# Moving two small TensorE groups in a recurrent attention step: the second selection of the new memory, and the masks of the second head half

## The chip, the core and the metric

The kernel runs on one NeuronCore of one Trainium2 chip. A core has a matrix engine (TensorE, "PE" in the profile, its weight loads "PEld"), three engines for elementwise work (VectorE "DVE", ScalarE "ACT", GpSimd "POOL"), a queue engine (SyncE "SP") that starts transfers, and two on-chip memories: SBUF, and PSUM, where matmuls put their sums. Each engine works through its own list of instructions in the order in which the program gives them; where one needs what another makes, it waits on a semaphore.

The metric is the time of one execution on the device, in microseconds. The trace is that of one further execution, taken with the hardware profiler.

## The reference

Two branches, mixed by a gate. Branch A is an attention layer over 2048 tokens with a recurrent memory: the tokens come in 64 segments of 32; each segment is preceded by 8 memory rows, and the layer's output for those 8 rows is the memory of the next segment. So the segments form a chain.

```python
for s in range(n_seg):                                   # 64
    xs = x[:, s * seg_len:(s + 1) * seg_len, :]          # 32 rows of 512
    h = jnp.concatenate([mem, xs], axis=1)               # 8 + 32 = 40 rows
    q = jnp.einsum('btd,dhe->bhte', h, Wq)               # 32 heads of 128
    k = jnp.einsum('btd,dhe->bhte', h, Wk)
    v = jnp.einsum('btd,dhe->bhte', h, Wv)
    scores = jnp.einsum('bhqe,bhke->bhqk', q, k) * scale
    scores = jnp.where(mask[None, None], scores, -1000000000.0)
    p = _softmax(scores, axis=-1)
    o = jnp.einsum('bhqk,bhke->bhqe', p, v)
    o = jnp.einsum('bhte,hed->btd', o, Wo)
    mem = o[:, :M, :]                                    # the next segment's memory
    outs.append(o[:, M:, :])
```

Branch B is a layer norm, a 512 x 1376 x 512 MLP with gelu, on the same tokens. The output is `g * a + (1 - g) * b` with `g = sigmoid(sum(x * gate_w))`. All tensors are bf16.

## The kernel before

**Two stages.** The first computes branch B for all tokens, block by block, and loads the attention's weights meanwhile; its result, already scaled by `1 - g`, goes to DRAM (`c_dr`). The second is a loop of 64 steps, one for a segment, written out in full. Four steps form a tile of 128 tokens: step `s` has tile `T = s // 4` and place `si = s % 4`. The order on every engine is that of the program text (`tc.manual_schedule()`); there is no planner. Some instructions are put off by hand: `act_q` holds casts for ScalarE and `dve_q` work for VectorE, and `flush` issues them at fixed places.

**What a step multiplies.** The activations are the stationary operand, 32 columns at a time, in one of four column tiles of the array; the weights stream past, 512 columns at a time. Four such matmuls, one for each column tile, are a **unit** (`qk_unit` L120, `v_unit` L139, `wo_group` L151). The stationary `hT` holds 24 of the segment's tokens and the 8 memory rows as `[128, KC, 32]`, with the 512 features in `KC = 4` blocks of 128. The other 8 tokens of each segment ("left") don't depend on the memory, so they are done for a whole tile ahead of time, as side work.

**A step in the order of TensorE:**

1. Projections: four groups (Q, K for the first half of the heads, then for the second) of four units each, one unit for each feature block `kc`, into PSUM banks `U[0]` to `U[3]` (L120). Unit `kc` needs block `kc` of `hT`. ScalarE casts each bank to `Tb` (L125), VectorE transposes it into `QT` or `KT` (L129).
2. `scores(s, 0)`: the scores of the first half of the heads, into `Sb[0]` in bank `SbF` (L257, L261), on top of masks that were put there earlier.
3. `mask_mm(1)`: four matmuls of 224 columns (L249) that put the masks of the second half into `Sb[1]` in bank `W`. The scores accumulate on them.
4. V's first half, four units into `X1` (L139), and the first unit of V's second half, into `X2`. ScalarE meanwhile takes the exponentials of the first scores (L693) and then copies `X1` out (L696).
5. `msum(0)`: sums over the leading columns of the exponentials (L268, L271); VectorE normalises them (L688, L689).
6. `scores(s, 1)`, onto the masks in `W`. ScalarE takes their exponentials in two parts (L681).
7. Two more units of V's second half, `msum(1)` (L268, L271), which needs the first of those two parts, the last unit of V, and ScalarE's copy of `X2` (L710).
8. `W1` side units, the column sums (`xsums`, L600), and `av` (L281, L286): exponentials times V. ScalarE copies the result out (`UT` L718, then `XR` L606).
9. `W2` side units, then `wo_pass`: eight units that multiply by Wo into bank `W` (L151). ScalarE copies the result to `w` in two halves of 256 columns (L633).
10. `mask_mm(0)`, `W3` side units, in some steps `out_sel`.
11. `new_mem`, twice. Each call is eight matmuls of 8 columns (L640) that pick the memory rows out of one half of `w` and turn them, and a VectorE copy of the result into two of the four blocks of the next `hT` (L642). The first call makes blocks 0 and 1 (bank `U[1]`), the second blocks 2 and 3 (bank `U[3]`).

The POOL engine multiplies the outputs of the tokens by their normalisation (L626) one step late; its factor comes back through DRAM. `wo_pass` of a step needs that product of the step before.

**Side work.** `side(T, si)` is a generator: `run(n)` issues `n` units of it, and a loop over `fill` issues the rest. At `si = 0` and `1` it is eight units of Q and K for the next tile's left tokens, at `si = 3` eight units of V for them, at `si = 2` the eight units of `wo_left` for the tile before. There is none at `si = 0, 1, 3` of the last tile and at `si = 2` of the first, so 60 steps have side work. `WS` gives `W1, W2, W3` as (3, 2, 0) for `si = 0` and (2, 2, 2) for the others; so three units, or two, are left when `new_mem` comes.

Of the kernel before, what the change touches and what calls it, by code (L numbers as in the profile page):

```python
# [27 lines left out]
def kernel(ctx, tc, A_x, A_mem0, A_Wq, A_Wk, A_Wv, A_Wo, A_seg_len, B_x, B_w1, B_b1, B_w2, B_b2, gate_w, out):  # L28
# [63 lines left out]
    def load_xT(T):  # L92
        xT = ew.tile([P, KC, P], BF16, tag="xT", bufs=3, name="xT")
        nc.sync.dma_start_transpose(out=xT[:], in_=x2[T * P:(T + 1) * P, :])
        xTs[T] = xT
# [7 lines left out]
    U = [lps.tile([P, 512], FP32, name=f"U{i}") for i in range(4)]  # L103
# [13 lines left out]
    def qk_unit(bk, G, t, hf, kc):  # L117
        h0, h1 = HF[hf]
        for j in range(4):
            nc.tensor.matmul(bk[32 * j:32 * j + 32, :], lhsT=G[:, kc, :], rhs=W5[t][:, kc, h0:h1, j, :],  # L120
                             start=(kc == 0), stop=(kc == KC - 1), tile_position=(0, 32 * j))

    def qk_cast(bk):
        Tb = ew.tile([P, 8, 32, 2], BF16, tag="Tb", bufs=3, name="Tb")
        nc.scalar.copy(out=Tb[:], in_=bk.rearrange("p (a b e) -> p a e b", a=8, b=2))  # L125
        return Tb

    def qk_tr(Tb, dst, hf, c0=0):
        nc.vector.transpose(out=dst[:, 8 * hf:8 * hf + 8, c0:c0 + 32, :].rearrange("p a r b -> p a (r b)").bitcast(FP32),  # L129
                            in_=Tb[:].rearrange("p a e b -> p (a e b)").bitcast(FP32))  # L130
# [6 lines left out]
    def v_unit(bk, G, vb, kc):  # L137
        for j in range(4):
            nc.tensor.matmul(bk[32 * j:32 * j + 32, :], lhsT=G[:, kc, :], rhs=Wv5[:, kc, 4 * vb:4 * vb + 4, j, :],  # L139
                             start=(kc == 0), stop=(kc == KC - 1), tile_position=(0, 32 * j))  # L140

    def v_out(V, vb):
        return V[:, 4 * vb:4 * vb + 4, :].rearrange("p i e -> p (i e)")
# [15 lines left out]
    def flush(q, n=1):  # L159
        for _ in range(min(n, len(q))):  # L160
            q.pop(0)()
# [17 lines left out]
    def vp_load(T, si):  # L179
        nc.sync.dma_start(VP[T % 2][:, si].rearrange("p v e -> p (v e)"), VLs[T][si:P:SPT].rearrange("p a v e -> p a (v e)"))  # L180
# [20 lines left out]
    def c_load(T):  # L201
        c = cw.tile([P, Dm], BF16, tag="c", name="c")
        nc.sync.dma_start(c[:], c_dr[T * P:(T + 1) * P, :])
        cs[T] = c
# [30 lines left out]
    def prep_h(s):  # L235
        T, si = divmod(s, SPT)
        nc.gpsimd.tensor_copy(out=hT[s % 3][:, :, 0:RIDE], in_=xTs[T][:, :, seg * si:seg * si + RIDE])
# [9 lines left out]
    def mask_mm(i2):  # L247
        for j in range(4):
            nc.tensor.matmul(Sb[i2][32 * j:32 * j + 32], lhsT=ident[:, 32 * j:32 * j + 32], rhs=Mk[:],  # L249
                             start=True, stop=True, skip_group_check=True, tile_position=(0, 32 * j))  # L250
# [315 lines left out]
    def run(n):  # L566
        for _ in range(n):
            next(fill, None)
# [5 lines left out]
    def side(T, si):  # L574
        gens = []
        if si == 2:
            if T >= 1:
                gens.append(wo_left(T - 1, X1))
        elif T + 1 < NT:
            gens = [[left_qk(T + 1, 0, 0, X1), left_qk(T + 1, 1, 0, X2)], [left_qk(T + 1, 0, 1, X1), left_qk(T + 1, 1, 1, X2)], [],  # L580
                    [left_v(T + 1, 0, X1), left_v(T + 1, 1, X2)]][si]
        return chain(*gens)
# [20 lines left out]
    def x_raw(s):  # L603
        XR = cw.tile([P, 4, NG, 32], BF16, tag="XR", name="XR")
        for j in range(4):
            nc.scalar.copy(out=XR[:, j], in_=U[j][:, 0:NG * 40].rearrange("p (i q) -> p i q", q=40)[:, :, 0:32])  # L606
        XRs[s] = XR
# [13 lines left out]
    def x_norm(s):  # L621
        T, si = divmod(s, SPT)
        XR, Rb = XRs.pop(s), Rbs.pop(s)[:].rearrange("p (c q) (h j) -> p h j c q", c=4, h=2)
        for out, o, a, b in ((UT[(s + 1) % 2], M, LEFT, 32), (UL[T % 2], LEFT * si, 0, LEFT)):
            for h in range(2):
                nc.gpsimd.tensor_tensor(out=out[:, :, 4 * h:4 * h + 4, o:o + b - a], in0=XR[:, :, 4 * h:4 * h + 4, a:b], in1=Rb[:, h, :, :, a:b], op=ALU.mult)  # L626
# [9 lines left out]
    def new_mem(w, hn, bk, k0):  # L636

        for k in (k0, k0 + 1):
            for c in range(4):
                nc.tensor.matmul(bk[32 * c:32 * c + 32, M * k:M * k + M], lhsT=w[:, k * P + 32 * c:k * P + 32 * c + 32], rhs=SelM[:],  # L640
                                 start=(k == k0), stop=True, skip_group_check=True, tile_position=(0, 32 * c))
        nc.vector.tensor_copy(out=hn[:, k0:k0 + 2, RIDE:32], in_=bk[:, M * k0:M * k0 + 2 * M].rearrange("p (k m) -> p k m", k=2))  # L642
# [3 lines left out]
    for s in range(nseg):  # L646
        T, si = divmod(s, SPT)
        last = s == nseg - 1
        hc, hn = hT[s % 3], hT[(s + 1) % 3]
        W1, W2, W3 = WS[si]  # L650
        fill = side(T, si)
        if s + 1 < nseg:
            prep_h(s + 1)
        if s >= 1:
            x_norm(s - 1)
        if si == 0 and T >= 2:
            c_load(T - 2)
        if si < 3:
            vp_load(T, si + 1)
        if last:  # L660
            c_load(T - 1)
            c_load(T)
        if si == 0 and T + 2 < NT:
            load_xT(T + 2)
        for n, (t, hf) in enumerate(((0, 0), (1, 0), (0, 1), (1, 1))):
            bk = U[n]
            for kc in range(KC):
                qk_unit(bk, hc, t, hf, kc)
            if n == 0:
                flush(act_q, 9)  # L670
                flush(dve_q, 9)
            qk_tr(qk_cast(bk[:]), (QT, KT)[t], hf, LEFT * (1 - t))
        V = cw.tile([P, NG, Dh], BF16, tag="V", name="V")
        E = cw.tile([P, NG, EW], BF16, tag="E", name="E")
        R = cw.tile([P, NG * 40], FP32, tag="R", name="R")
        Rs[s] = R
        xsum = SbF[:, 0:32 * NG].rearrange("p (i q) -> p i q", q=32)

        def exps(i2, x):
            c = slice(0, 40) if x else slice(40, EW)  # L680
            nc.scalar.activation(out=E[:, 4 * i2:4 * i2 + 4, c], in_=Sb[i2][:, :, c], func=ACTF.Exp, scale=scale)  # L681

        def msum(i2):
            sums(U[i2][:, 320:352].rearrange("p (i q) -> p i q", q=8), E[:, 4 * i2:4 * i2 + 4, :], 40, 48, 8, True)

        def mnorm(i2):
            r, e = RP[i2], E[:, 4 * i2:4 * i2 + 4, 40:56].rearrange("p i (a q) -> p i a q", q=8)
            nc.vector.reciprocal(out=r, in_=U[i2][:, 320:352])  # L688
            nc.vector.tensor_tensor(out=e, in0=e, in1=r.rearrange("p (i q) -> p i q", q=8).unsqueeze(2).to_broadcast([P, 4, 2, 8]), op=ALU.mult)  # L689

        scores(s, 0)
        mask_mm(1)
        nc.scalar.activation(out=E[:, 0:4, :], in_=Sb[0], func=ACTF.Exp, scale=scale)  # L693
        for kc in range(KC):
            v_unit(X1, hc, 0, kc)
        nc.scalar.copy(out=v_out(V, 0), in_=X1[:])  # L696
        v_unit(X2, hc, 1, 0)
        if not last:
            msum(0)
            mnorm(0)  # L700
        scores(s, 1)
        for i2 in range(2):
            exps(1, i2)
        for kc in range(1, 3):
            v_unit(X2, hc, 1, kc)
        if not last:
            msum(1)
            mnorm(1)
        v_unit(X2, hc, 1, 3)
        nc.scalar.copy(out=v_out(V, 1), in_=X2[:])  # L710
        if last:
            break
        run(W1)
        xsums(s, E)
        recip_x(s)
        av(s, V, E)
        for j in (0, 2, 1, 3):
            nc.scalar.copy(out=UT[s % 2][:, j, :, 0:M], in_=U[j][:, 0:NG * 40].rearrange("p (i q) -> p i q", q=40)[:, :, 32:40])  # L718
        x_raw(s)
        run(W2)  # L720
        prep_q(s + 1)
        w = wo_pass(UT[s % 2], 2)
        if s >= 1:
            ws[s - 1] = w
        mask_mm(0)
        run(W3)
        for _ in extra(T, si):
            pass
        new_mem(w, hn, U[1], 0)
        for _ in fill:  # L730
            pass
        new_mem(w, hn, U[3], 2)
        if si == 3 and T + 2 < NT:
            left_x(T + 2)
        flush(dve_q, 9)
        nc.vector.tensor_tensor(out=rmin[:, 0:RW], in0=rmin[:, 0:RW], in1=R[:, 0:RW], op=ALU.min)
        flush(act_q, 9)
# [163 lines left out]
```

## Time and profile before

| | us |
|---|---|
| median of 3 runs | 787.48 |
| lowest, highest | 785.29, 788.54 |
| profiled execution | 785.75 |
| its span | 784.0 |
| TensorE busy | 766.3 (98%) |
| ScalarE busy | 524.5 (67%) |
| VectorE busy | 341.2 (44%) |
| POOL busy | 278.8 (36%) |

The span goes from the first instruction of the profiled execution to its last; the execution's own time is 1.75 us longer. The loop of steps begins about 97 us into it. Busy times of TensorE are unions of matmuls whose ends are modelled: matmuls overlap, so a wait shorter than their tail does not show as idle time, and the starts of successive matmuls have to be read instead. A row of the timeline gives start, length (both in us), engine, line, operation, tiles, shape and the number of merged instructions; in brackets, where there is one, the idle time before it and what ended it.

### The profile page before, as it was taken

How to read it: one execution, taken by the hardware profiler on the slowest of the kernel's cores; microseconds unless marked ns; L12 is line 12 of the kernel's file. 1: busy time of each engine (PE TensorE's matmuls, PEld its weight loads, DVE VectorE, ACT ScalarE, POOL GpSimd, SP SyncE). 2: the span in 40 equal slices, each digit the busy share in tenths (PEclk: the TensorE clock that was granted, in tenths of full speed). 3: DMA queues.
4: the chain of work that ended last, by engine and by line, in shares of the span. 5: the costliest groups of instructions: out<-in, count | busy, mean ns of one | idle time of the engine just before them, and what ended most of it. 6: DMA issues, size and time to landing. Idle time of an engine off the chain costs nothing.

```text
span 784.0 us, 44302 instructions
## 1 busy us (share of the span) xinstructions
PE 766.3 (98%) x19673; PEld 416.6 (53%) x19687; DVE 341.2 (44%) x1235; ACT 524.5 (67%) x1439; POOL 278.8 (36%) x523
## 2 busy tenths in 40 slices
PE   7999999999999999999999999999999999999996
PEld 5666455555555555555555555555555555555553
DVE  5776244334334343434443433434343444434334
ACT  4666566667677676667667677766666767666663
POOL 4111034333344343344434424443334443342342
PEclk9999999999999999999999999999999999999999
DMA  6789311213121222212121212122221212221211
GB/s 199 271 256 387 119 57 61 74 61 88 61 61 62 78 71 77 72 58 74 49 88 61 88 62 74 60 67 70 78 72 57 80 43 88 62 80 62 67 63 44
DMA packets 53174, 70.61 MB, mean 90 GB/s; under 512 B 21289, under 2 KB 42898, under 8 KB 51442
## 3 DMA queue, kind: packets, MB, share of 16 engines
q1 hardware_dynamic: 51250, 64.84, 25.6%
q8 instruction: 156, 2.56, 1.3%
q0 software_dynamic: 784, 1.97, 0.7%
q10 hardware_dynamic: 944, 0.92, 0.4%
q14 instruction: 40, 0.33, 0.1%
HBM read 56.96 MB, written 4.45 MB: 78 GB/s over the span
## 4 chain that ended last, share of the span: by engine, by line
PE 87%; DVE 1%; issue 0%; ACT 0%; DVEq 0%
PE U L120 30%; PE X L139 18%; PE W L151 15%; PE X L120 7%; PE X L151 4%; PE U L281 3%; PE U L640 2%; PE U L268 1%; PE W L257 1%; PE SbF L257 1%; PE W L249 1%; PE SbF L600 1%; PE SbF L249 1%; PE U L286 1%; PE U L466 1%; PE U L221 0%
## 5 line engine op out<-in xcount | busy, mean ns | idle before, releaser
L626 POOL TENSOR_TENSOR UT<-XR,Rb 128x384 bf16<-128x384 bf16 x126 | 140.3, 1134 | 297.6 <-DMA Rb<-r_dr 237.6
L125 ACT CAST Tb<-U 128x512 bf16<-128x512 f32 x258 | 150.9, 585 | 86.6 <-PE U L120 85.6
L120 PEld LDWEIGHTS <-hT 128*32 128x32 bf16 x4096 | 98.3, 96 | 110.9 <-DVE hT L642 26.8
L139 PE MATMUL X<-Wv_sb,hT 128*32 128x512 bf16 x2048 | 145.7, 379 | 0.0
L120 PE MATMUL U<-Wq_sb,hT 128*32 128x512 bf16 x2048 | 139.9, 381 | 0.8 <-DVE hT L642 0.5
L120 PE MATMUL U<-Wk_sb,hT 128*32 128x512 bf16 x2048 | 132.7, 379 | 0.0
L151 PE MATMUL W<-Wo_sb,UT 128*32 128x512 bf16 x2080 | 124.8, 380 | 1.5 <-ACT UT L718 1.5
L642 DVE CAST hT<-U 128x16 bf16<-128x16 f32 x126 | 22.0, 175 | 222.7 <-PE U L640 222.4
L129 DVE STREAM_TRANSPOSE QT<-Tb 128x256 f32<-128x256 f32 x128 | 56.6, 443 | 78.4 <-ACT Tb L125 78.4
L151 PEld LDWEIGHTS <-UT 128*32 128x32 bf16 x2080 | 57.8, 96 | 57.7 <-issue 18.5
L606 ACT CAST XR<-U 128x256 bf16<-128x256 f32 x252 | 78.6, 438 | 0.0
L129 DVE STREAM_TRANSPOSE KT<-Tb 128x256 f32<-128x256 f32 x128 | 57.1, 446 | 44.5 <-ACT Tb L125 44.3
L633 ACT CAST w<-W 128x256 bf16<-128x256 f32 (+1 forms) x128 | 41.9, 378 | 46.5 <-PE W L151 46.5
L139 PEld LDWEIGHTS <-hT 128*32 128x32 bf16 x2048 | 53.1, 95 | 20.4
L618 POOL TENSOR_TENSOR racc<-racc,R 128x72 f32<-128x72 f32 x63 | 21.2, 336 | 111.7 <-PE U L286 79.3
L626 POOL TENSOR_TENSOR UL<-XR,Rb 128x128 bf16<-128x128 bf16 x126 | 60.3, 502 | 0.0
L718 ACT CAST UT<-U 128x64 bf16<-128x64 f32 x252 | 35.3, 227 | 28.3 <-PE U L286 28.3
L710 ACT CAST V<-X 128x512 bf16<-128x512 f32 x64 | 37.4, 585 | 22.3 <-PE X L139 22.1
L466 PE MATMUL U<-w_sb,hTm 128*128 128x512 bf16 (+1 forms) x163 | 49.2, 379 | 0.6
L696 ACT CAST V<-X 128x512 bf16<-128x512 f32 x64 | 37.4, 585 | 15.6 <-PE X L139 15.6
L460 PEld LDWEIGHTS <-w_sb 128*128 128x128 bf16 (+1 forms) x352 | 34.2, 101 | 20.3 <-issue 3.0
L640 PEld LDWEIGHTS <-w 128*32 128x32 bf16 x1008 | 20.7, 94 | 42.6 <-ACT w L633 29.3
(158 smaller groups left out, 1179.8 us busy)
## 6 DMA issues: line engine op xcount, KB each, us to landing
Rb<-r_dr SPq DMA_DIRECT2D x63, 512.0 KB, 3.8
Wv_sb<-in_A_Wv_dram SPq DMA_DIRECT2D x4, 1024.0 KB, 6.5
Wq_sb<-in_A_Wq_dram SPq DMA_DIRECT2D x4, 1024.0 KB, 7.0
Wk_sb<-in_A_Wk_dram SPq DMA_DIRECT2D x4, 1024.0 KB, 9.5
Wo_sb<-in_A_Wo_dram SPq DMA_DIRECT2D x4, 1024.0 KB, 15.0
VP<-VL SPq DMA_DIRECT2D x64, 64.0 KB, 3.2
c<-c_dr SPq DMA_DIRECT2D x16, 128.0 KB, 3.3
out_dram<-o SPq DMA_DIRECT2D x16, 128.0 KB, 2.1
```

Source lines behind the costliest of these rows:

```text
L120: nc.tensor.matmul(bk[32 * j:32 * j + 32, :], lhsT=G[:, kc, :], rhs=W5[t][:, kc, h0:h1, j, :], start=(kc == 0), stop=(kc == KC - 1), tile_ ...
L125: nc.scalar.copy(out=Tb[:], in_=bk.rearrange("p (a b e) -> p a e b", a=8, b=2))
L129: nc.vector.transpose(out=dst[:, 8 * hf:8 * hf + 8, c0:c0 + 32, :].rearrange("p a r b -> p a (r b)").bitcast(FP32), in_=Tb[:].rearrange("p ...
L139: nc.tensor.matmul(bk[32 * j:32 * j + 32, :], lhsT=G[:, kc, :], rhs=Wv5[:, kc, 4 * vb:4 * vb + 4, j, :], start=(kc == 0), stop=(kc == KC - ...
L151: nc.tensor.matmul(bk[32 * c:32 * c + 32, :], lhsT=U_[:, j, i, :], rhs=Wo_sb[:, 4 * i + j, :], start=(n == 0), stop=(n == NW - 1), tile_po ...
L466: nc.tensor.matmul(bp(blk, tt)[:], lhsT=hTm[blk % 2][:rows, fc, tt * P:(tt + 1) * P], rhs=w2_sb[:rows, fc, :], start=(fc == 0), stop=(fc = ...
L606: nc.scalar.copy(out=XR[:, j], in_=U[j][:, 0:NG * 40].rearrange("p (i q) -> p i q", q=40)[:, :, 0:32])
L626: nc.gpsimd.tensor_tensor(out=out[:, :, 4 * h:4 * h + 4, o:o + b - a], in0=XR[:, :, 4 * h:4 * h + 4, a:b], in1=Rb[:, h, :, :, a:b], op=ALU ...
L633: nc.scalar.copy(out=w[:, a:a + Dm // parts], in_=W[:, a:a + Dm // parts])
L640: nc.tensor.matmul(bk[32 * c:32 * c + 32, M * k:M * k + M], lhsT=w[:, k * P + 32 * c:k * P + 32 * c + 32], rhs=SelM[:], start=(k == k0), s ...
L696: nc.scalar.copy(out=v_out(V, 0), in_=X1[:])
L710: nc.scalar.copy(out=v_out(V, 1), in_=X2[:])
```

## The change

Two groups of TensorE instructions change their place in each step.

- The masks of the second half of the heads, `mask_mm(1)`, stood between the first scores and V's first half. They now stand behind V's first half, ahead of the first unit of V's second half.
- The second `new_mem` (blocks 2 and 3 of the next `hT`) stood behind all side units that were left. It now stands behind one of them; the rest follow it.

No instruction is added or taken away, and no operand changes. In steps without side work the second edit changes nothing.

```diff
         scores(s, 0)
-        mask_mm(1)
         nc.scalar.activation(out=E[:, 0:4, :], in_=Sb[0], func=ACTF.Exp, scale=scale)
         for kc in range(KC):
             v_unit(X1, hc, 0, kc)
+        mask_mm(1)
         nc.scalar.copy(out=v_out(V, 0), in_=X1[:])
         v_unit(X2, hc, 1, 0)
...
         new_mem(w, hn, U[1], 0)
+        run(1)
+        new_mem(w, hn, U[3], 2)
         for _ in fill:
             pass
-        new_mem(w, hn, U[3], 2)
         if si == 3 and T + 2 < NT:
             left_x(T + 2)
```

## The prediction, made before the changed kernel was run

> **What bounds the kernel now.** I read the page first, then the waits of the weight loads, then stretches of the timeline.
>
> ```profile
> span 784.0 us, 44302 instructions
> PE 766.3 (98%) x19673; PEld 416.6 (53%) x19687; DVE 341.2 (44%) x1235; ACT 524.5 (67%) x1439; POOL 278.8 (36%) x523
> ```
>
> TensorE carries the kernel: 98% busy, and no other engine is near. But busy PE is a modelled overlap, so small stalls between matmuls vanish in it. They show at the weight loads, which carry the semaphore waits:
>
> ```profile
> PEld L640 <- ACT w L633: 29.3, 66, 0.8
> PEld L120 <- DVE hT L642: 26.8, 66, 0.8
> ```
>
> Columns: total us, times, longest. Two waits come back in nearly each of the 64 steps: L640 (the selection of the new memory) waits for ScalarE's copy of w, and L120 (next step's projections) for VectorE's copy of the new memory into hT. Edit B touches just these; a third stall, at the place of edit A, shows further down. I looked at both places in time.
>
> **Edit B, the second selection earlier.** The end of step 28 and its neighbour, step 29, show both forms; first step 29 (tile 7, si = 1), where two side units stand between the two selections:
>
> ```profile
> 413.65 0.62 PE L120 MATMUL X<-Wk_sb,GL 128*32 128x512 bf16 x8
> 414.21 0.21 PE L640 MATMUL U<-SelM,w 128*32 128x8 bf16 x8
> 414.27 0.60 PE L120 MATMUL X<-Wk_sb,GL 128*32 128x512 bf16 x8
> 414.70 0.20 PE L640 MATMUL U<-SelM,w 128*32 128x8 bf16 x8
> 414.79 1.15 PE L120 MATMUL U<-Wq_sb,hT 128*32 128x512 bf16 x16
> 415.76 0.60 PE L120 MATMUL U<-Wk_sb,hT 128*32 128x512 bf16 x8
> ```
>
> Beside it, the weight loads of hT, VectorE's copies into hT and ScalarE's copies of w:
>
> ```profile
> 414.78 0.12 PEld L120 LDWEIGHTS <-hT 128*32 128x32 bf16 x8
> 415.32 0.12 PEld L120 LDWEIGHTS <-hT 128*32 128x32 bf16 x8 [0.41 <-DVE hT L642]
> ```
>
> ```profile
> 414.56 0.17 DVE L642 CAST hT<-U 128x16 bf16<-128x16 f32 x1 [3.10 <-PE U L640]
> 415.09 0.17 DVE L642 CAST hT<-U 128x16 bf16<-128x16 f32 x1 [0.36 <-PE U L640]
> ```
>
> ```profile
> 413.79 0.65 ACT L633 CAST w<-W 128x256 bf16<-128x256 f32 x2 [0.65 <-PE W L151]
> ```
>
> Read starts, not durations (the durations of matmuls overlap). The middle of the step gives the pace of an unhindered unit of four 512-wide matmuls:
>
> ```profile
> 408.03 0.27 PE L249 MATMUL W<-Mk,ident 128*32 128x224 bf16 x4
> 408.13 1.25 PE L139 MATMUL X<-Wv_sb,hT 128*32 128x512 bf16 x20
> 409.21 0.19 PE L268 MATMUL U<-E,BO 128*32 128x32 bf16 x4
> 409.24 0.19 PE L271 MATMUL U<-E,BO 128*32 128x32 bf16 x4
> 409.26 0.27 PE L257 MATMUL W<-QT,KT 128*32 128x40 bf16 x16
> 409.37 0.20 PE L261 MATMUL W<-QT,KL 128*32 128x64 bf16 x4
> 409.40 0.63 PE L139 MATMUL X<-Wv_sb,hT 128*32 128x512 bf16 x8
> 409.98 0.20 PE L268 MATMUL U<-E,BO 128*32 128x32 bf16 x4
> ```
>
> Five units from 408.13 to 409.21 make 0.216 us a unit. The 16 matmuls on the new hT should take 0.86; from 414.79 to 415.76 they take 0.97. The loss is the wait for hT's second half: the second selection starts at 414.70, its VectorE copy ends at 415.26, the load that needs it goes at 415.32, 0.06 later. After the edit one side unit stands between the selections: 414.27 + 0.216 = 414.49. Is the second half of w there? ScalarE's pair ends at 413.79 + 0.65 = 414.44, and with the same 0.06 for the signal 414.50: just in time. A step with no side units measures it directly:
>
> ```profile
> 128.67 0.12 PEld L640 LDWEIGHTS <-w 128*32 128x32 bf16 x8 [0.75 <-ACT w L633]
> 128.94 0.12 PEld L640 LDWEIGHTS <-w 128*32 128x32 bf16 x8 [0.15 <-ACT w L633]
> ```
>
> ```profile
> 129.25 1.05 PE L120 MATMUL U<-Wq_sb,hT 128*32 128x512 bf16 x16
> 130.12 0.39 PE L120 MATMUL U<-Wk_sb,hT 128*32 128x512 bf16 x4
> ```
>
> There the second selection follows 0.27 after the first, with nothing between; 414.21 + 0.27 = 414.48. So the new wait is zero, the margin about zero too. Then: selection 0.07 (414.21 to 414.27, rounded up, as its loads can't be fetched ahead), the last side unit 0.216, which ends at 414.78, exactly when hT's first half is ready (the load at 414.78 now), so the projections start at 414.79 as today. Their third unit comes at 415.22; hT's second half, by the first copy's lag (414.21 to 414.56, then 0.17, 0.06), at 414.49 + 0.58 = 415.07. No stall. The 16 matmuls take 0.87 instead of 0.97, as they do in the step without side units (129.25 to 130.12): **0.10 us** a step. Step 28 has si = 0: three units between the selections, after the edit one, and two behind:
>
> ```profile
> 403.61 0.82 PE L120 MATMUL X<-Wk_sb,GL 128*32 128x512 bf16 x12
> ...
> 405.31 0.60 PE L120 MATMUL U<-Wk_sb,hT 128*32 128x512 bf16 x8
> ```
>
> ```profile
> 405.59 0.58 ACT L125 CAST Tb<-U 128x512 bf16<-128x512 f32 x1 [0.47 <-PE U L120]
> ```
>
> Selection at 403.83, two units from 403.90 to 404.33, 16 matmuls to 405.19 instead of 405.31: **0.12 us**. Side units exist in 60 steps: si = 0, 1, 3 of the first 15 tiles, si = 2 of the last 15. 45 x 0.10 + 15 x 0.12 = **6.3 us**. Both ends: nothing if w's second half is 0.10 late; below nothing beyond that (the slower rival below); 7.9 at most if the projections also began without their 0.03 of delay (414.79 against 414.70 + 0.06; 60 x 0.13). I take 6.3: the step without side units shows both halves of it.
>
> What else moves: VectorE and ScalarE issue in the same order. The side tile's last cast starts some 0.06 later on ScalarE; what follows it there waits 0.47 for TensorE (the 405.59 row), so that's covered, and uncovered would cost those 0.06. No DMA, SP or POOL instruction is moved. The POOL product that wo_pass (L151) needs is early:
>
> ```profile
> 406.19 2.23 POOL L626 TENSOR_TENSOR UT<-XR,Rb 128x384 bf16<-128x384 bf16 x2 [4.27 <-ACT Tb L125]
> ```
>
> It ends at 408.42. wo_pass is eight units (1.73), and ScalarE copies its result from 413.79 on, so it starts before 412; about 3 us of cover, from which a step shorter by 0.2 takes little.
>
> **Edit A, the masks behind V's first half.** The same four matmuls take 0.10 (408.03 to 408.13), so on TensorE it is a swap: V's first half ends 0.10 earlier, L268 at 409.21 and the second scores at 409.26 stay. What it moves is ScalarE:
>
> ```profile
> 408.13 0.59 ACT L125 CAST Tb<-U 128x512 bf16<-128x512 f32 x1 [0.23 <-PE U L120]
> 408.61 0.36 ACT L693 ACTIVATE E<-SbF 128x224 bf16<-128x224 f32 x1
> 409.22 0.58 ACT L696 CAST V<-X 128x512 bf16<-128x512 f32 x1 [0.24 <-PE X L139]
> 409.70 0.43 ACT L681 ACTIVATE E<-W 128x64 bf16<-128x64 f32 x2
> 410.48 0.58 ACT L710 CAST V<-X 128x512 bf16<-128x512 f32 x1 [0.35 <-PE X L139]
> 411.47 0.56 ACT L718 CAST UT<-U 128x64 bf16<-128x64 f32 x4 [0.41 <-PE U L286]
> ```
>
> A 512-wide cast is followed 0.48 later by the next activation (408.13 to 408.61). V's copy at 409.22 is followed 0.48 later, with no idle time, by L681, the exps of the second half: ScalarE, not the scores, sets that start. And L681 is on the path: the two V units from 409.40 end at 409.83, but the sums L268 stand at 409.98, 0.15 late, waiting for E. With V's copy at 409.12, ScalarE is free at 409.60. When do the scores allow it? Their last matmuls (L261) start at 409.37 to 409.38. For the lag of such a 64-wide matmul to ScalarE I take av's last ones, to the copy L718 at 411.47 that waits for them:
>
> ```profile
> 411.12 0.27 PE L281 MATMUL U<-E,V 32*128 32x40 bf16 x16
> 411.23 0.20 PE L286 MATMUL U<-E,VP 32*128 32x64 bf16 x4
> ```
>
> From 411.23 to 411.47 is 0.24, so 409.62. L681 moves from 409.70 to 409.62: **0.08 us**. The sums move to 409.90 (0.07 of wait stays), V's last unit and its copy (410.48) with them. That copy ends at 411.06 and releases the second half of av at 411.12, so the gain isn't eaten there. It applies in the 63 steps before the last: **5.0 us**. Ends: zero, if something unseen sets L681; 0.095 a step or 6.0 if the cast alone does. A loss is excluded: nothing but the masks moves back, and they are done about 0.2 before the second scores.
>
> The Trainium skill (ScalarE: Activation LUTs, What ACT_TABLE_LOAD costs) has an activation with immediates at 186 + 0.833 N ns, back-to-back ones overlapping by 93: an estimate of 0.52 us for this cast where the rows have 0.48. By it L681 would come at 409.64 and edit A be worth 3.8 us; the rows decide.
>
> **The sum.** 6.3 + 5.0 = 11.3 us. The profiled execution took 785.75, so 774.4. It lies under the median of the other three, 787.48; from the mean of the four, 786.8, I get **775.5 us**.
>
> **Rivals.**
> Only B pays (L681 is held by something other than the cast): 786.8 - 6.3 = 780.5. Against: 0.48 twice and no idle time before L681.
> Only A pays (B's 0.10 is given back at the first scores, L257, by casts and transposes): 781.8. Against: the casts and transposes ahead of those scores wait for these projections (the 405.59 row: idle until TensorE), so they move along.
> Slower: the second selection waits for w. TensorE takes matmuls in order, so a late w holds the last side unit and all behind it. Each 0.01 us later than 414.49 costs 0.6 us in all; at 0.10 B is gone, and from 0.19 (11.3 / 60) on the kernel is slower; a copy behind one more 0.48 cast on ScalarE would give 0.48 - 0.19, times 60, 804 us. For it: the margin is nil. Against: the 0.27 of the bare step. The Trainium skill (TensorE: Matmul & The Clock Gate, Part 3: Packing small matmuls) says that matmuls start and end in strict program order; the rows agree, as the side unit behind L640 starts only at 414.27.
> No change: both edits lie beside the path. Against: the 0.97 and the 0.15 are stalls of TensorE itself.
>
> **How the numbers follow.** Both pay 0.75; only B 0.09; only A 0.07; no change 0.04; slower 0.05. A measurement can tell about 0.5%, 3.9 us; the first three are faster by more: 0.91, 0.04, 0.05. The low end takes the upper terms (6.0 + 7.9 from 786.8 is 772.9); the high end takes in both single cases: 772.5 to 781.9.
>
> **What would show it.** The 16 matmuls on hT at 0.87; the second L640 some 0.28 behind the first; the wait of L120 for hT falling from 26.8 to a few us; L681 0.08 closer to the scores; L268 0.08 earlier; the selections of two neighbouring steps 0.18 to 0.20 closer together. The prediction is wrong if L640's wait for w grows by several us, or if new waits appear at L257 or L281.

## The result, and the profile after

The changed kernel takes **779.97 us** (median of 6 runs, 779.49 to 782.41); the kernel before, run beside it, 786.99 (6 runs). The ratio is 0.9915, interval 0.9904 to 0.9926: 7.0 us less, where 11.3 were forecast. The time lies in the range given, but only because the range takes in the rivals' times: it stands at "only B pays" (780.5), not at the forecast of 775.5.

The profile's first lines, of the kernel after:

```profile
span 777.7 us, 44316 instructions
PE 761.1 (98%) x19687; PEld 420.3 (54%) x19687; DVE 345.1 (44%) x1235; ACT 529.5 (68%) x1439; POOL 278.7 (36%) x523
```

The profiled execution took 779.49, against 785.75 before. TensorE is still the bound, and again the starts have to be read.

**Edit B came out as worked out.** The timeline of TensorE at the end of step 29, and the loads and copies beside it:

```profile
411.31 0.62 PE L120 MATMUL X<-Wk_sb,GL 128*32 128x512 bf16 x8
411.88 0.22 PE L640 MATMUL U<-SelM,w 128*32 128x8 bf16 x8
411.94 0.39 PE L120 MATMUL X<-Wk_sb,GL 128*32 128x512 bf16 x4
412.15 0.21 PE L640 MATMUL U<-SelM,w 128*32 128x8 bf16 x8
412.21 0.39 PE L120 MATMUL X<-Wk_sb,GL 128*32 128x512 bf16 x4
412.45 1.05 PE L120 MATMUL U<-Wq_sb,hT 128*32 128x512 bf16 x16
413.32 0.60 PE L120 MATMUL U<-Wk_sb,hT 128*32 128x512 bf16 x8
```

```profile
412.15 0.12 PEld L640 LDWEIGHTS <-w 128*32 128x32 bf16 x8
...
412.45 0.12 PEld L120 LDWEIGHTS <-hT 128*32 128x32 bf16 x8 [0.15 <-DVE hT L642]
412.74 0.47 PEld L120 LDWEIGHTS <-hT 128*32 128x32 bf16 x12 [0.17 <-DVE hT L642]
```

The second selection stands 0.27 to 0.28 behind the first (411.88, 412.15), with one side unit between. Its load shows no wait for `w`. From 412.45 to 413.32 the 16 matmuls on the new `hT` take 0.87; they took 0.97. The weight loads' waits say the same:

```profile
PEld L640 <- ACT w L633: 29.3, 66, 0.8
...
PEld L268 <- issue: 16.5, 64, 0.3
PEld L120 <- DVE hT L642: 16.3, 95, 0.5
```

The wait of L120 for `hT` fell from 26.8 to 16.3 us, not to a few: the number of waits rose from 66 to 95, because the first half of `hT` is now waited for as well (0.15 in the rows above). The second half's load still shows 0.17, yet it costs nothing: it goes at 412.74, and its matmuls, the third unit, start at 412.89. L640's wait for `w` is unchanged at 29.3.

**Edit A moved the cast, and almost nothing behind it.** ScalarE and TensorE in the middle of step 29, after:

```profile
406.80 0.58 ACT L696 CAST V<-X 128x512 bf16<-128x512 f32 x1
407.37 0.42 ACT L681 ACTIVATE E<-W 128x64 bf16<-128x64 f32 x2
408.14 0.58 ACT L710 CAST V<-X 128x512 bf16<-128x512 f32 x1 [0.35 <-PE X L139]
```

```profile
406.57 0.27 PE L249 MATMUL W<-Mk,ident 128*32 128x224 bf16 x4
406.67 0.39 PE L139 MATMUL X<-Wv_sb,hT 128*32 128x512 bf16 x4
...
406.94 0.27 PE L257 MATMUL W<-QT,KT 128*32 128x40 bf16 x16
407.04 0.20 PE L261 MATMUL W<-QT,KL 128*32 128x64 bf16 x4
407.07 0.63 PE L139 MATMUL X<-Wv_sb,hT 128*32 128x512 bf16 x8
407.64 0.20 PE L268 MATMUL U<-E,BO 128*32 128x32 bf16 x4
```

V's copy now starts 0.24 ahead of the last scores (406.80, 407.04); it was 0.15 (409.22, 409.37). L681 used to follow the copy by 0.48; it now follows it by 0.57. From the last scores to L681 there are 0.33, and there were 0.33 before (409.37 to 409.70). The sums L268 stand 0.60 behind the scores (it was 0.61), and between the two V units that start at 407.07 and the sums the same hole is left. The wait of the sums' weight loads, called "issue" since the profile names no releaser, was this before:

```profile
PEld L268 <- issue: 17.4, 64, 0.3
```

It fell to 16.5, so by 0.9 us in all 64 steps. Edit A was to bring 5.0.

**The step as a whole.** From the starts of the first scores of successive steps in each trace, the usual length of a step in ns (median of the undisturbed ones), and the sum of what single steps of 8 to 59 lie above it (by over 70 ns):

```
                 si = 1,2,3   si = 0   lying above, us
before              10453      10815    2.6 (7 steps)
after               10334      10664    3.2 (13 steps)
```

45 x 0.119 + 15 x 0.151 = 7.6 us, less 0.6 us for more stops, is 7.0. The stops are those of one profiled execution each, so that this equals the difference of the medians to the tenth is in part luck: the two profiled executions differ by 6.3. What the stops are is taken up below.

### The profile page after: what moved, and what is told of

Its sections match the earlier page's. It is cut to its first block, busy times and chain, and to the rows that moved or that the text cites. A ratio compares the mean times of both kernels' runs of the same rounds, so it can differ in the third digit from the quotient of the medians.

```text
span 777.7 us, 44316 instructions
## 1 busy us (share of the span) xinstructions
PE 761.1 (98%) x19687; PEld 420.3 (54%) x19687; DVE 345.1 (44%) x1235; ACT 529.5 (68%) x1439; POOL 278.7 (36%) x523
## 4 chain that ended last, share of the span: by engine, by line
PE 87%; DVE 1%; ACT 0%; issue 0%; DVEq 0%
PE U L120 29%; PE X L139 18%; PE W L151 15%; PE X L120 8%; PE X L151 4%; PE U L281 3%; PE U L640 2%; PE U L268 1%; PE W L257 1%; PE SbF L257 1%; PE W L249 1%; PE SbF L600 1%; PE SbF L249 1%; PE U L286 1%; PE U L466 1%; PE U L221 0%
## 5 line engine op out<-in xcount | busy, mean ns | idle before, releaser
L120 PEld LDWEIGHTS <-hT 128*32 128x32 bf16 x4096 | 104.6, 96 | 109.3 <-DVE hT L642 16.3
L139 PE MATMUL X<-Wv_sb,hT 128*32 128x512 bf16 x2048 | 151.2, 379 | 0.0
L120 PE MATMUL U<-Wq_sb,hT 128*32 128x512 bf16 x2048 | 133.3, 380 | 0.5 <-DVE hT L642 0.2
L120 PE MATMUL U<-Wk_sb,hT 128*32 128x512 bf16 x2048 | 132.7, 379 | 0.0
L151 PEld LDWEIGHTS <-UT 128*32 128x32 bf16 x2080 | 59.4, 96 | 55.6 <-issue 16.3
L466 PE MATMUL U<-w_sb,hTm 128*128 128x512 bf16 (+1 forms) x176 | 52.7, 383 | 0.0
L125 ACT CAST Tb<-X 128x512 bf16<-128x512 f32 x62 | 36.9, 595 | 7.8 <-PE X L120 6.0
```

The costliest lines, as they stand in the source:

```text
L151: nc.tensor.matmul(bk[32 * c:32 * c + 32, :], lhsT=U_[:, j, i, :], rhs=Wo_sb[:, 4 * i + j, :], start=(n == 0), stop=(n == NW - 1), tile_po ...
L466: nc.tensor.matmul(bp(blk, tt)[:], lhsT=hTm[blk % 2][:rows, fc, tt * P:(tt + 1) * P], rhs=w2_sb[:rows, fc, :], start=(fc == 0), stop=(fc = ...
```

## The experiments

**Each edit alone.** Only B: the masks back at their old place.

```diff
         scores(s, 0)
+        mask_mm(1)
         nc.scalar.activation(out=E[:, 0:4, :], in_=Sb[0], func=ACTF.Exp, scale=scale)
         for kc in range(KC):
             v_unit(X1, hc, 0, kc)
-        mask_mm(1)
```

> The second selection behind one side unit, the masks at their old place. The prediction's working for this part gives 6.3 us less than before (45 steps x 0.10 and 15 x 0.12), with the 16 matmuls on hT at 0.87 us. The trace of the changed kernel shows that part to hold as worked out, so both theories below expect about 0.8% less than before, and L681 0.48 us behind V's copy as before.

Only A: the second selection back behind the side units.

```diff
         new_mem(w, hn, U[1], 0)
-        run(1)
-        new_mem(w, hn, U[3], 2)
         for _ in fill:
             pass
+        new_mem(w, hn, U[3], 2)
```

> The masks behind V's first half, the second selection at its old place. The prediction gave 5.0 us less than before for it. From the trace of the changed kernel, where the sums L268 came only 0.014 us earlier, both theories expect 63 x 0.014 = 0.9 us, 0.1%, which can hardly be told from nothing; L681 0.57 us behind V's copy instead of 0.48.

Measured: only B 780.39 (0.9924, 0.9911 to 0.9937), only A 785.99 (0.9995, 0.9986 to 1.0005) against 786.61; the interval of only A includes no change at all, so A has to be read from the steps. The usual steps, in ns: 10349 and 10678 with B, 10441 and 10803 with A. So B is worth 45 x 0.104 + 15 x 0.137 = 6.7 us, A 63 x 0.012 = 0.8, and the two add up. What remains is why A pays a sixth of its term.

**What sets the second exps, L681?** Theory 1: still the cast of V; theory 2: the scores, which need longer to reach ScalarE than was taken. Two kernels move the cast and leave the scores. In the first, the masks are cut by columns, one half ahead of V's first half and one behind (`mask_mm` takes a range of columns there).

```diff
+        mask_mm(1, 0, 2)
         nc.scalar.activation(out=E[:, 0:4, :], in_=Sb[0], func=ACTF.Exp, scale=scale)
         for kc in range(KC):
             v_unit(X1, hc, 0, kc)
-        mask_mm(1)
+        mask_mm(1, 2, 4)
```

> The changed kernel with the masks of the second half cut in two by columns: 112 columns ahead of V's first half, 112 behind it, so that V's copy on ScalarE comes 0.047 us later than in the changed kernel and as much earlier than before. Theory 1 (an activation can follow a 512-wide cast after 0.48 us only if what it waits for is there by then; if it misses that, it starts when the cast is nearly over, 0.57 behind its start; in the changed kernel the scores come about 0.01 us after that point): the point moves 0.047 back, the scores are there, L681 starts 0.48 behind V's copy, 0.04 earlier than in the changed kernel, and the step is 0.03 to 0.04 shorter: some 2 us less than the changed kernel. Theory 2 (the scores themselves let L681 start no earlier than 0.32 us after their last matmul, whatever ScalarE does): L681 stays where it was in the changed kernel, 0.53 behind V's copy, and the time too.

In the second, the kernel after with V's cast cut in two, the second half behind the first part of the exps:

```diff
-        nc.scalar.copy(out=v_out(V, 0), in_=X1[:])
+        nc.scalar.copy(out=v_out(V, 0)[:, 0:256], in_=X1[:, 0:256])
...
-        for i2 in range(2):
-            exps(1, i2)
+        exps(1, 0)
+        nc.scalar.copy(out=v_out(V, 0)[:, 256:512], in_=X1[:, 256:512])
+        exps(1, 1)
```

> The changed kernel with ScalarE's copy of V's first half cut in two by columns: 256 columns ahead of the first part of the second exps, 256 between that part and the second. ScalarE is then free well before the scores are done. Theory 1: L681's first part starts 0.24 us after the last scores matmul, 0.08 earlier than in the changed kernel, the sums L268 as much, and 63 x 0.077 = 4.9 us are gained: about 775 us. Theory 2: L681 stays 0.32 behind the scores, and the time is that of the changed kernel within 1 us.

Measured: 781.18 (0.9935, 0.992 to 0.995) and 780.22 (0.9922, 0.9907 to 0.9936). The timeline of ScalarE and TensorE in step 30 with the cast cut in two:

```profile
417.14 0.37 ACT L696 CAST V<-X 128x256 bf16<-128x256 f32 x1
417.71 0.22 ACT L681 ACTIVATE E<-W 128x64 bf16<-128x64 f32 x1 [0.20 <-PE W L261]
417.83 0.37 ACT L703 CAST V<-X 128x256 bf16<-128x256 f32 x1
```

```profile
417.38 0.20 PE L261 MATMUL W<-QT,KL 128*32 128x64 bf16 x4
...
417.99 0.20 PE L268 MATMUL U<-E,BO 128*32 128x32 bf16 x4
```

ScalarE is idle for 0.20 and the bracket names the scores, yet L681 stays 0.33 behind them and the sums 0.61. Theory 1 falls. With half the masks ahead, L681 stands 0.52 behind the cast and where it was (1.79 into the step).

**How long do the scores take to reach ScalarE, and why?** Both kernels have the cut cast, and leave out score matmuls of the second half (L257): all 16, or 8.

```diff
-        for i in range(4 * i2, 4 * i2 + 4):
+        for i in range(4 * i2, 4 * i2 + (4 if i2 == 0 else 0)):
```

> On the kernel with V's copy cut in two (ScalarE free early), the 16 matmuls of 40 columns of the second half's scores are left out (its output is not the reference's); only the four of 64 columns are left, about 0.10 us earlier than before. It asks what sets L681, which stood at 1.79 us behind the first scores matmul of the step whatever ScalarE did. Theory 2a (a fixed lag of 0.32 us from the last scores matmul to ScalarE): L681 at 1.37 + 0.32 = 1.69. Theory 2b (the small matmuls are issued faster, 25 ns for four, than the array works them off, so the recorded starts run ahead by some 15 ns for each four; without such a queue the lag is 0.24 to 0.25, as the last step shows where TensorE paused before the last of them): 1.37 + 0.25 + 0.01 to 0.03 = about 1.63. Theory 2c (something at a fixed time, VectorE's work on the other half of E for one): 1.79.

The other has 2 in place of the 0.

> The same with 8 of the 16 matmuls left out (its output is not the reference's). The last scores matmul comes 0.05 us earlier than in the full kernel, at 1.42. Theory 2a: L681 at 1.74. Theory 2b: 1.42 + 0.25 + 0.03 to 0.05 = about 1.71. Theory 2c: 1.79.

One time each: 770.28 and 774.05, beside 787.26. ScalarE and TensorE in step 30 without any of the 16, then with 8:

```profile
413.54 0.22 ACT L681 ACTIVATE E<-W 128x64 bf16<-128x64 f32 x1
```

```profile
413.24 0.20 PE L261 MATMUL W<-QT,KL 128*32 128x64 bf16 x4
```

```profile
413.96 0.22 ACT L681 ACTIVATE E<-W 128x64 bf16<-128x64 f32 x1
```

```profile
413.64 0.20 PE L261 MATMUL W<-QT,KL 128*32 128x64 bf16 x4
```

In ns from the first scores of the step to the last of the four L261 and to L681:

```
                        last L261   L681   between
all 16 (cut cast)            1470   1789       319
8                            1420   1722       302
none                         1370   1656       286
```

So L681 moves with the scores, which a fixed time (2c) excludes. But the lag isn't fixed either (2a): the four matmuls take 25 ns to issue, and L681 comes 33 ns earlier for each four left out. A lag that grows with the small matmuls queued ahead (2b) has the direction, at half the size, 8 ns and not 15 for each four. Nor does it go to 0.24 without them; but in the usual step the eight matmuls of `msum(0)` still stand ahead of the scores. The last step has no `msum(0)`. There the last L261 is 0.246 ahead of L681 in the kernel after, where TensorE happens to pause among the four, and 0.247 in both kernels with scores left out, without a pause:

```profile
753.03 0.20 PE L261 MATMUL W<-QT,KL 128*32 128x64 bf16 x4
```

```profile
753.29 0.22 ACT L681 ACTIVATE E<-W 128x64 bf16<-128x64 f32 x1
```

(These rows are of the kernel without any of the 16; the last of the four starts at 753.039, L681 at 753.286.) In the four kernels that have all 16 there and no pause it is 0.263 to 0.265. So about 0.247 is what is left with few small matmuls ahead, and more of them lengthen it. That is 2b's direction again; but leaving out `msum(0)` alone was not run, and `av`, where 16 small matmuls stand ahead of L286, still has 0.24, with another tile shape (32*128) and a copy as the reader. What makes the difference stays open; that L681 hangs on the scores, 0.32 behind them, does not. The Trainium skill (TensorE: Matmul & The Clock Gate, The cost: per-tile semaphore tail) has a tail of this direction: where every small matmul signals its end, the signals follow each other at 26.3 ns. If each of the 16 signalled, leaving them out would move L681 by an estimated 0.42 us; the trace has 0.13, so a tail of that size isn't there.

**Is one side unit the right number?** Without it the second selection stands directly behind the first:

```diff
         new_mem(w, hn, U[1], 0)
-        run(1)
+        run(0)
         new_mem(w, hn, U[3], 2)
```

> The changed kernel with the second selection directly behind the first, no side unit between. The copy of w's second half releases it 0.27 us after the first, so TensorE should stand about 0.21 us there with the side units behind it; the two (three) units then separate the selection from the projections, and nothing waits for hT. Worked out: each of the 60 steps 0.20 us longer than in the changed kernel, 12 us in all, so about 792 us, some 5 us slower than before. If TensorE could run the side units past the waiting selection, the time would be that of the changed kernel.

Measured: 790.56 (1.0043, 1.0028 to 1.0058), slower than before by 0.4%. The end of step 29, weight loads and matmuls:

```profile
418.19 0.12 PEld L640 LDWEIGHTS <-w 128*32 128x32 bf16 x8 [0.43 <-ACT w L633]
418.47 0.12 PEld L640 LDWEIGHTS <-w 128*32 128x32 bf16 x8 [0.15 <-ACT w L633]
```

```profile
418.20 0.49 PE L640 MATMUL U<-SelM,w 128*32 128x8 bf16 x16
418.53 0.60 PE L120 MATMUL X<-Wk_sb,GL 128*32 128x512 bf16 x8
```

The second selection waits for the copy of `w` and stands 0.28 behind the first, as it does with the unit between; both side units wait behind it. The usual step is 0.19 (si = 0: 0.22) longer than after. By the Trainium skill (TensorE: Matmul & The Clock Gate, Part 3: Packing small matmuls) matmuls start and end in strict program order, and this trace agrees. The slower rival's mechanism is thus real; it begins one unit further forward, and with one unit the margin is nil, as was said.

**A version that takes the hole.** If L681 can't come earlier, TensorE can be given something else ahead of the sums that need it. The last V unit is cut by columns, one half ahead of `msum(1)`, on top of the kernel after (`v_unit` takes a range of column blocks there):

```diff
         for kc in range(1, 3):
             v_unit(X2, hc, 1, kc)
         if not last:
+            v_unit(X2, hc, 1, 3, 0, 2)
             msum(1)
             mnorm(1)
-        v_unit(X2, hc, 1, 3)
+        v_unit(X2, hc, 1, 3, 2, 4)
```

> The changed kernel with the last unit of V's second half cut in two by columns (256 each), one half ahead of the sums L268 of the second half, the other behind them. In the changed kernel the sums stand 0.138 us by the recorded starts, waiting for E. If the recorded starts are true (theory 2a or 2c), 0.108 us of work fits whole into that wait: the copy of V's second half and the second half of av come 0.108 earlier, 63 x 0.108 = 6.8 us, about 773 us. If the recorded starts run ahead of the array by about 0.075 us at that place (theory 2b), only 0.06 of the wait is real: the gain is 63 x 0.06 = 4 us, about 776 us, and the sums come 0.04 later than in the changed kernel.

Measured: **777.24** (0.9878, 0.986 to 0.9896), the best of all, and all four runs (777.12 to 777.87) lie below the lowest of the kernel after. Step 30, TensorE and ScalarE, with the cut unit:

```profile
417.28 0.20 PE L261 MATMUL W<-QT,KL 128*32 128x64 bf16 x4
417.32 0.74 PE L139 MATMUL X<-Wv_sb,hT 128*32 128x512 bf16 x12
417.88 0.20 PE L268 MATMUL U<-E,BO 128*32 128x32 bf16 x4
...
417.94 0.29 PE L139 MATMUL X<-Wv_sb,hT 128*32 128x256 bf16 x4
```

```profile
418.27 0.58 ACT L711 CAST V<-X 128x512 bf16<-128x512 f32 x1 [0.25 <-PE X L139]
```

(The row at 417.32 counts the half unit among its 12.) The sums stay 0.60 behind the scores; V's second copy stands 0.99 behind them, where in the kernel after it is 1.10 (407.04, 408.14). The half unit fits whole into the hole, with none of the 0.04 of delay that 2b foresaw. The usual step is 10229 (si = 0: 10557), 0.105 and 0.107 shorter, 6.6 us over the 63 steps that have the cut. Only 2.7 of it reached the median. In the profiled executions, stops took 5.9 us where the kernel after has 3.2, which accounts for 2.7; and the first scores of the loop stand at 102.78 us, where the kernel after has them at 101.53. These 1.25 us lie ahead of the changed code. In the other profiled executions this start lies anywhere from 101.0 to 103.2, which speaks for scatter and not for a price of the cut.

**What are the stops?** In nearly each step that is too long, TensorE stands still at a place where the profile names no releaser ("issue") or a mere gap shows between two matmuls, and 66 of 79 such stops in the five kernels of the table below with 593 instructions or more end 1.2 to 1.75 us after a 16 KB packet of the instruction queue has landed. One packet lands about every 4.5 us, so chance alone would put an eighth of them there. Most packets are followed by no stop. A step has 593 TensorE instructions (609 at si = 0), with the cut unit 8 more. Theory F: TensorE runs through the short instructions (sums, xsums, av) faster than its program is brought in. Theory G: the stops have nothing to do with that supply. By theory F, instructions that cost nothing in the step itself should cost time. The kernel after with 8, or 16, unused matmuls of 8 columns ahead of `msum(1)`, where TensorE waits anyway:

```diff
+            for k in range(2):
+                for j in range(4):
+                    nc.tensor.matmul(U[2][32 * j:32 * j + 32, 400 + 8 * k:408 + 8 * k],
+                                     lhsT=BO[:, 32 * j:32 * j + 32], rhs=Mk[:, 0, 0:8],
+                                     start=True, stop=True, ...
             msum(1)
```

> The same with 8 such matmuls, 16 instructions a step. Theory F: between the changed kernel and the one with 16, some 781 to 785 us. Theory G: 780 within 1 us.

The other has `range(4)`.

> The changed kernel with 16 matmuls of 8 columns a step that nothing uses (with their weight loads 32 instructions, 5% more of TensorE's program), in the place where TensorE waits 0.138 us for E ahead of the sums of the second half. The kernel with V's last unit cut in two put 0.108 us of work there without moving the sums; these take about 0.10, so a usual step stays at 10.33 us. What it asks: whether the irregular stops of TensorE (3 us in all in the changed kernel, 6 in the one with V's last unit cut in two, 1.4 where 32 instructions a step were left out; nearly each ends about 1.4 us after a 16 KB packet of the instruction queue has landed) come from the supply of TensorE's program. If so (theory F), more instructions in the same time make them longer and more frequent: several us more than the changed kernel, 783 to 790 us, at an unchanged usual step. If they don't come from there (theory G), the time stays at 780 within 1 us.

Measured: 783.93 (0.996, 0.9947 to 0.9973) and 791.22 (1.0061, 1.0038 to 1.0085), beside 786.89. So 16 unused matmuls take back the whole gain and more. The same place of step 30, with 16:

```profile
421.98 0.21 PE L261 MATMUL W<-QT,KL 128*32 128x64 bf16 x4
422.02 0.63 PE L139 MATMUL X<-Wv_sb,hT 128*32 128x512 bf16 x8
422.45 0.28 PE L709 MATMUL U<-Mk,BO 128*32 128x8 bf16 x16
422.59 0.20 PE L268 MATMUL U<-E,BO 128*32 128x32 bf16 x4
```

They fit into the hole: the sums stand 0.61 behind the scores, as without them. The usual step is 10336 against 10334, and at si = 0 the undisturbed steps are 10661 to 10672, as after; but only 5 of 13 are left undisturbed, with 8 unused matmuls and with 16. What grew is the stops; the longest, in step 12:

```profile
232.66 0.40 PE L120 MATMUL X<-Wq_sb,GL 128*32 128x512 bf16 x4
232.89 0.39 PE L120 MATMUL X<-Wk_sb,GL 128*32 128x512 bf16 x3
234.17 0.39 PE L120 MATMUL X<-Wk_sb,GL 128*32 128x512 bf16 x1 [0.90 <-issue]
```

From 232.90 to 234.17 no matmul starts, in the midst of one unit, whose operands other matmuls of it have already read. The kernel after has the same at the same kind of place, half as long:

```profile
440.39 0.38 PE L120 MATMUL X<-Wk_sb,GL 128*32 128x512 bf16 x1
441.10 0.40 PE L120 MATMUL X<-Wk_sb,GL 128*32 128x512 bf16 x3 [0.34 <-issue]
```

The packet before this stop landed at 439.59, the one before the stop of 234.17 at 232.88: 1.51 and 1.29 ahead. By dose, steps 8 to 59:

```
                    instructions          stops   us in all   median us
                    a step    per us
before               593       56.7         7        2.6        786.99
after                593       57.4        13        3.2        779.97
last V unit cut      601       58.8        16        5.9        777.24
8 unused matmuls     609       58.9        17        5.7        783.93
16 unused matmuls    625       60.5        26       11.5        791.22
16 scores left out   561       55.0         6        1.3        770.28
```

With 16 unused matmuls, steps 8 to 59 took 8.3 us more in the profiled execution than after, and 11.5 - 3.2 = 8.3 is all stops. The steps ahead of and behind these took 1.7 more; the profiled executions differ by 9.65 (789.14, 779.49). That more TensorE instructions, at the same usual step, mean more and longer stops is shown. The number in a step is not all, since before and after have the same number and 7 and 13 stops. What orders the six, to 0.2 us, is the number for each microsecond of the usual step: the same program in a shorter step has to come faster. The six other profiled executions, at 56.2 to 58.1, have 1.7 to 4.1 us of stops. (Each figure is that of one execution.) The packets follow TensorE's instructions, too. This is the queue after, and with 16 unused matmuls:

```profile
q8 instruction: 156, 2.56, 1.3%
```

```profile
q8 instruction: 164, 2.69, 1.4%
```

Eight packets more for 63 x 32 = 2016 instructions more are 252 instructions a packet, so this queue carries TensorE's program. All this is as theory F has it, and G's 780 within 1 us is excluded. That the packet's arrival ends the stops is still a reading of when they end: no run changed the supply itself, and why 1.4 us lie between is open.

## Why the prediction was right or wrong

- **Faster, in the range:** right in sign, half too large. The sum had 11.3; the steps gave 7.6, and 0.6 went to stops. That the time still fell into the range is owed to its high end, which took in both single cases.
- **Edit B, 6.3 us:** right, 6.7 measured (0.104 and 0.137 a step, 0.10 and 0.12 taken). The pieces held: 0.28 between the selections, no new wait for `w`, 16 matmuls in 0.87. The margin of nil held as well, as the kernel with no unit between shows. (Its upper end, 60 x 0.13, is 7.8 and not 7.9.)
- **Edit A, 5.0 us:** wrong. The failed step is "From 411.23 to 411.47 is 0.24, so 409.62. L681 moves from 409.70 to 409.62". Taken the same way, the lag behind L261 is 0.33, and 409.37 + 0.33 = 409.70: L681 was already where the scores allow it. The 0.48 behind V's cast, without idle time, was true too. In the trace before the two came within 5 ns of each other (cast: its start at 1314 and 482 more, 1796 ns into the step; scores: the last L261 at 1472 and the 319 of the kernel after, 1791; L681 at 1796), so removing one gained next to nothing. The lag of 0.24 was borrowed from the end of av; the runs without scores show that the lag of L261 itself is not one number, 0.286 to 0.319 in the usual step.
- **"A loss is excluded" for A:** held. The masks are done in time, and no wait at L257 or L281 appeared.
- **"L120's wait for `hT` falls to a few us":** wrong (16.3). As a sign of the stall it was badly chosen, since the loads here wait ahead of need (412.74 for matmuls at 412.89); the matmuls' starts were the right sign.
- **"Only B pays", 0.09:** this came about, for the reason named in it (L681 is held by something other than the cast). The trace of before could not tell it from the forecast: 0.48 behind the cast and 0.33 behind the scores fit both. One borrowed lag was all that told them apart, and should have cost A more than 9 in 100.
- **Not foreseen:** the stops. They are small in this change, but they took 2.7 of the 6.6 us that the cut V unit saved in the steps.

## What to carry to other kernels

An instruction that starts the moment one predecessor ends may still have a second predecessor that ends at the same moment; before a gain is counted, work out each release by itself, with the lag of that very pair of instructions, and count only the distance to the second. On an in-order engine, a consumer placed as early as its operand allows gains its whole wait, and one unit further forward it holds up everything behind it. Where TensorE is 98% busy with short matmuls, their number is a cost of its own: a cut that fills a hole with more, smaller instructions can lose in stops part of what it wins in the step (2.7 of 6.6 us here).

## What the hardware showed that was not expected

- Unused matmuls inside a wait, which leave the usual step at 10.336 us, cost 4 us (8 a step) and 11 us (16 a step) by the medians. In steps 8 to 59 of the profiled executions 2.5 and 8.3 us of this are stops, most of which end some 1.4 us behind a 16 KB packet of the instruction queue.
- The time from a 64-column matmul to the ScalarE activation that waits for it was 0.286, 0.302 or 0.319 us in step 30, with 0, 8 or 16 of the L257 in front of the four, and 0.245 to 0.265 in the last step, which has no sums ahead of the scores, of all runs but the kernel before, where V's cast sets the start.
